# The first round of a top-32 search, over 144 columns instead of 168

## The chip, the cores and the metric

The kernel runs on one core of one Trainium2 chip, in float32. Its metric is the device time of one execution in microseconds (us). The engines are called PE (TensorE), DVE (VectorE), ACT (ScalarE), POOL (GpSimd) and SP (SyncE); PEld is the weight loading of PE.

## The reference

Attention that keeps, for each query, only the scores that reach its 32nd largest one, and then a layer of experts in which each token goes to one expert.

```python
scores = scale * np.matmul(q, k.transpose(0, 1, 3, 2))      # B, H, S, D = 8, 8, 576, 64
kth = np.partition(scores, -32, axis=-1)[..., -32:-31]
scores = np.where(scores >= kth, scores, -1e9)
attn = softmax(scores)
x = np.matmul(attn, v)                                      # to 4608 rows of 512
expert = np.argmax(x @ w_gate, axis=1)                      # 8 experts
y = np.maximum(x @ w1[expert], 0) @ w2[expert]              # 512 -> 1024 -> 512
out = gate_weight[:, None] * y
```

## The kernel before

**The steps.** A tile is 128 queries of one head against its 576 keys. The attention is a list of 144 steps (`work`); a step handles two tiles (index `m`), 18 steps make a batch, and 8 batches follow each other. The main loop (from L916) goes over the steps under an order of PE, ACT and DVE that is written out by hand; SP and POOL follow the order of the program. Work is staggered: PE multiplies queries and keys (L276) and ACT copies the scores to `s` (L283) three steps ahead, so four buffers of `s` are in turn; DVE folds the scores of step i + 1 while it searches step i; PE transposes the weights of step i - 1 (`transposed`, L398 to L419).

**The search.** What DVE must find is the 32nd largest of 576 scores per query. First the scores are folded. `fold` (L290, L292) takes the larger and the smaller of each two scores, into `h` and `l` (288 columns each). `fold_on` (L298, L300) does the same once more with `h`: the larger ones go to the first 144 columns of `few` (QF = 144), the smaller ones to `hl`. `few` has 168 columns (LW): behind the 144 lie three lists of eight, the eight largest of `l` and of each half of `hl` (MAX8, L329). Whatever is among the 32 largest of the tile is then among the 168, unless a list was too short; `doubts` (L360, on POOL) compares the last entry of each list with the threshold, and in the rare case an exact path at the end of the program does all again.

`search` then takes four rounds of eight. In each, MAX8 (L338) writes the eight largest values of its source to `tops`; after each but the last, MATCH_REPLACE8 (L345, with a MATCH_VALUE_LOAD of the eight values in front of it) puts a very low number in their places. Before the change round 0 reads all 168 columns of `few` and the replacement writes to `scr`; rounds 1 to 3 read `scr`. Both tiles of a step go through each round one after the other. Before the last scan the loop calls `fold_on` for the next step (`then`). The threshold is the last of the 32 values.

**What follows a search.** ACT turns the thresholds into `low` (L354), then makes from `s` a huge number where a score lies under the threshold (`depths`, L370); POOL subtracts that from the scores (`less`, L379); ACT takes the exponential with its sum (`weights`, L387), with a bias that POOL made from the first maximum (`nbias`, L342). PE transposes the weights in the next step and ACT copies them out (L402 to L419). Every few steps PE multiplies them with the values (L432), ACT copies the result (L434), PE turns it to rows (L443), ACT copies it (L450), ACT and DVE make the divisors (`rz`, L454 to L457), and POOL multiplies rows by divisors (L478). At the end of a batch small DVE operations choose experts and places (L488 to L534) and a table of blocks (L587 to L626); they are put between the scans one at a time (`tick`).

**The experts.** From the second batch on, pieces of expert blocks (L687, L702) are put into PE's order between the attention's steps, as many at each step as a credit allows; it counts steps and blocks, not time. The blocks that are left over run after the attention, on PE almost alone.

**Buffers.** `few` has three, `scr` one, `s` four. DVE's instructions run in their order; semaphores of DVE's own guard a value that its next instruction reads.

Of the kernel before, what the change touches and what calls it, by code (L numbers as in the profile page):

```python
# [30 lines left out]
def _inner(ap: bass.AP, n: int) -> bass.AP:  # L31
    return _ins(ap, len(ap.ap), n)
# [3 lines left out]
def kernel(  # L36
# [6 lines left out]
    moe_w2: bass.AP,  # L43
    out: bass.AP,
):

# [46 lines left out]
    QF = S // 4  # L95
# [23 lines left out]
    k = SimpleNamespace()  # L119
# [48 lines left out]
    for odd in range(2):  # L168
        for h in range(2):
            r = slice(h * D, (h + 1) * D)  # L170
# [63 lines left out]
    def in_turn(put):  # L234

        if not k.exact:
            tc.keep_in_program_order(put)
        return put
# [11 lines left out]
    def tails(tiles):  # L250
        return tiles[0][1] == 2 * NC
# [52 lines left out]
    def tick():  # L304

        while aside:
            if next(aside[0], "end") != "end":
                return
            aside.pop(0)
# [7 lines left out]
    def search(tiles, s, f, then=lambda: None):  # L317

        m_all = range(2)
        tops = k.small.tile([P, 2, TOP_K], F32, name="tops", bufs=4)  # L320
        if k.exact:
            src = [s[:, m, :, :].rearrange("p j k -> p (j k)") for m in m_all]
            width = S
        else:
            src = [f.few[:, m, :] for m in m_all]
            width = LW
            for m in m_all:
                for j, away in enumerate((f.l[:, m, :], f.hl[:, m, 0:QF // 2], f.hl[:, m, QF // 2:QF])):
                    nc.vector.max(out=f.few[:, m, QF + 8 * j:QF + 8 * j + 8], in_=away)  # L329
        scr = k.att.tile([P, 2, width], F32, name="scr", bufs=1)  # L330
        nbias = k.small.tile([P, 2], F32, name="nbias", bufs=3)
        R = TOP_K // 8

        for r in range(R):
            if r == R - 1:
                then()
            for m in m_all:
                nc.vector.max(out=tops[:, m, r * 8:(r + 1) * 8], in_=src[m])  # L338
                if r:
                    tick()  # L340
            if r == 0:
                in_turn(nc.gpsimd.tensor_scalar_mul(nbias, tops[:, :, 0], -scale))  # L342
            if r < R - 1:
                for m in m_all:
                    nc.vector.match_replace(  # L345
                        out=scr[:, m, :], in_to_replace=tops[:, m, r * 8:(r + 1) * 8],
                        in_values=src[m], imm_value=NEG,
                    )
                    if r:
                        tick()  # L350
                    src[m] = scr[:, m, :]
        thr = tops[:, :, TOP_K - 1]
        low = k.small.tile([P, 2], F32, name="low", bufs=3)
        nc.scalar.activation(low, thr, AF.Copy, scale=STEEP)  # L354

        def doubts():
            n, i = tiles[0]
            at = n.b * U + n.u
            over = doubt[:, at:at + 2, 2 * NC, :] if tails(tiles) else doubt[:, at, 2 * i:2 * i + 2, :]
            k.last_pool = in_turn(nc.gpsimd.tensor_tensor(  # L360
                over, f.few[:, :, QF + 7:LW:8], _inner(thr, NL), op=ALU.subtract
            )).ins

        return low, nbias, doubts
# [115 lines left out]
    def choice(lg):  # L480

        r = SimpleNamespace(lg=lg)
        mx = k.small.tile([P, KC], F32, name="mx")
        r.oh = oh = k.small.tile([P, KC, E], F32, name="oh")
        idx = k.small.tile([P, KC], F32, name="idx")

        def steps():
            nc.vector.tensor_reduce(mx, lg, axis=AX.X, op=ALU.max)  # L488
            yield
            nc.vector.tensor_tensor(oh, lg, _inner(mx[:, :], E), op=ALU.is_ge)  # L490
            yield
            nc.vector.tensor_tensor(oh, oh, _ins(e_less[:, :], 1, KC), op=ALU.mult)
            yield
            nc.vector.tensor_tensor(lg, lg, _inner(mx[:, :], E), op=ALU.subtract)
            yield
            nc.vector.tensor_reduce(idx, oh, axis=AX.X, op=ALU.min)
            yield
            nc.vector.tensor_tensor(oh, e_same, _inner(idx[:, :], E), op=ALU.is_equal)
            yield

        r.steps = steps()
        return r
# [231 lines left out]
    with fast:  # L734
# [171 lines left out]
        def loop():  # L906
# [9 lines left out]
            for i, (b, g) in enumerate(work):  # L916
# [8 lines left out]
                if i + 1 < len(work):  # L925
                    f_of[i + 1] = fold(s_of[i + 1])
                    then = lambda: fold_on(f_of[i + 1])
                low, nbias, doubts = search(tiles, s_of[i], f_of.pop(i), then)
                at_place("small")
                w_of[i] = depths(s_of[i], low)  # L930
# [73 lines left out]
    with ExitStack() as outer:  # L1004
# [10 lines left out]
        with ExitStack() as st:  # L1015
# [7 lines left out]
            with tc.For_i(0, B, 1) as b:  # L1023
# [3 lines left out]
                for u in range(0, U, 2):  # L1027
                    two = [load_unit(b, u), load_unit(b, u + 1)]
                    for n in two:
                        load_values(n)  # L1030
                        open_unit(n)
                    for g in groups(u):
                        tiles = [(two[a - u], tile) for a, tile in g]
                        s, steps = scores(products(tiles))
                        for step in steps:
                            step()
                        low, nbias, _ = search(tiles, s, None)
                        w = depths(s, low)
                        less(s, w)
                        weights(tiles, w, nbias)  # L1040
                        for _ in transposed(tiles, w):
                            pass
                        n, tile = tiles[0]
                        if tile == (NC - 1 if n.u % 2 else 2 * NC):
                            for _ in outputs(n, x):
                                pass
                            for _ in divisors(n):
                                pass
                            logits(n, lg)
                            rows(n, x)  # L1050
                r = choice(lg)
# [68 lines left out]
```

## Time and profile before

| what | us |
|---|---|
| median of 6 runs | 1373.19 (1371.40 to 1375.38) |
| the profiled execution | 1374.58 |
| its span, first to last instruction | 1373.0 |
| PE busy | 1234.4 (90%) |
| PE weight loads | 837.8 (61%) |
| DVE busy | 1085.7 (79%) |
| ACT busy | 931.2 (68%) |
| POOL busy | 661.1 (48%) |

Busy times are shares of the whole span. The attention fills roughly the first four fifths of it and the experts that are left the last fifth, in which DVE has next to nothing to do, so 79% of the span is nearly all of the attention. A group of instructions is told as its line, engine, operation, output and input with their shapes, and count, then the busy time in us and the mean length of one in ns, then the idle time of the engine ahead of it. Instructions of DVE overlap a little: the next one starts before the one ahead of it is shown as ended.

### The profile page before, as it was taken

Reading aid. Unit: us, or ns where it says so; the run is one execution under the profiler, and the core shown is the slowest. Engines: PE = TensorE matmul, PEld = TensorE weight load, DVE = VectorE, ACT = ScalarE, POOL = GpSimd, SP = SyncE. Lnnn points to the kernel's source line nnn. Section 1 sums busy time; section 2 is a strip of 40 time slices with the busy share of each in tenths; the row PEclk is TensorE's granted clock in tenths of the full one; section 3 lists DMA queues with packets and bytes.
Section 4 is the critical chain, followed back from the end, with each engine's and each line's share of the span. In section 5 each row is a group of like instructions: output and inputs, shape, how many; then the busy total and the mean of one; then the engine's idle time right before and its main releaser. Section 6 shows DMA issues by size and latency. Waiting matters only on the chain. (4 is left out here: it accounts for less than half of the span.)

```text
span 1373.0 us, 24487 instructions
## 1 busy us (share of the span) xinstructions
PE 1234.4 (90%) x7666; PEld 837.8 (61%) x7666; DVE 1085.7 (79%) x4591; ACT 931.2 (68%) x2113; POOL 661.1 (48%) x805
## 2 busy tenths in 40 slices
PE   5777677677799999999999999999999999999995
PEld 3444444344466666766666666767676676776773
DVE  8999999999999999999999999999999820000000
ACT  4788877877888888888877788887777821111110
POOL 3454557555654666566556656565557621000000
PEclk9788887887899999999999999999999999999998
DMA  2000011001583267427654474357542759999890
GB/s 82 29 29 29 28 36 55 29 29 44 179 290 122 94 231 266 140 73 255 232 176 166 168 274 145 113 190 296 178 167 88 294 182 361 385 322 331 302 320 18
DMA packets 102220, 231.68 MB, mean 169 GB/s; under 512 B 5182, under 2 KB 25918, under 8 KB 102080
## 3 DMA queue, kind: packets, MB, share of 16 engines
q1 hardware_dynamic: 95328, 209.76, 43.5%
q0 software_dynamic: 6464, 19.97, 4.0%
q8 instruction: 62, 1.02, 0.3%
q14 instruction: 78, 0.64, 0.1%
q10 hardware_dynamic: 288, 0.30, 0.1%
HBM read 208.72 MB, written 22.33 MB: 168 GB/s over the span
## 5 line engine op out<-in xcount | busy, mean ns | idle before, releaser
L379 POOL TENSOR_TENSOR w<-s,w 128x576 f32<-128x576 f32 x288 | 409.1, 1440 | 433.7 <-ACT w L370 433.7
L687 PE MATMUL ph<-xTs,w 128*128 128x128 f32 x2560 | 308.6, 276 | 6.7 <-ACT xTs L664 6.0
L687 PEld LDWEIGHTS ph<-xTs,w 128*128 128x128 f32 x2560 | 297.4, 192 | 27.3 <-issue 19.9
L702 PE MATMUL py<-w,hT 128*128 128x512 f32 x640 | 292.2, 596 | 0.0
L338 DVE MAX8 tops<-scr 128x8 f32<-128x168 f32 x864 | 247.8, 320 | 0.0
L276 PE MATMUL sc<-qkb 64*128 64x288 f32 (+1 forms) x1280 | 223.0, 474 | 9.6 <-ACT s L283 5.2
L387 ACT ACTIVATE w<-w,nbias 128x576 f32<-128x576 f32 x288 | 224.1, 792 | 3.5 <-POOL w L379 2.5
L370 ACT ACTIVATE w<-s,low 128x576 f32<-128x576 f32 x288 | 207.6, 768 | 4.7
L398 PE MATMUL wTm<-turn,w 128*128 128x128 f32 x1152 | 170.9, 288 | 28.9 <-ACT xl L450 17.1
L999 DVE CAST any_i<-pd 1x1 int32<-1x1 f32 x1 | 0.1, 146 | 237.2 <-PE pd L997 237.2
L398 PEld LDWEIGHTS wTm<-turn,w 128*128 128x128 f32 x1152 | 132.7, 146 | 89.7 <-issue 36.2
L702 PEld LDWEIGHTS py<-w,hT 128*128 128x128 f32 x640 | 114.4, 190 | 117.6 <-issue 116.5
L345 DVE MATCH_REPLACE8 scr<-tops,scr 128x168 f32<-128x168 f32 x576 | 178.4, 316 | 0.0
L283 ACT COPY s<-sc 128x576 f32<-128x576 f32 x288 | 169.0, 641 | 11.2 <-PE sc L276 11.2
L404 ACT COPY wT<-wTm 128x512 f32<-128x512 f32 x256 | 139.1, 604 | 38.9 <-PE wTm L398 38.7
L276 PEld LDWEIGHTS sc<-qkb 64*128 64x128 f32 (+1 forms) x1280 | 119.0, 197 | 73.7 <-issue 27.0
L432 PE MATMUL po<-wT,vb 128*64 128x288 f32 x1024 | 156.9, 455 | 0.4 <-ACT wTt L419 0.4
L708 POOL DMA_INDIRECT out_dram<-y,xg x40 | 43.1, 1077 | 212.7 <-ACT y L716 199.7
L329 DVE MAX8 few<-l 128x8 f32<-128x288 f32 x288 | 128.8, 447 | 0.0
L432 PEld LDWEIGHTS po<-wT,vb 128*64 128x64 f32 x1024 | 75.2, 152 | 78.5 <-issue 29.0
L290 DVE TENSOR_TENSOR h<-s 128x576 f32<-128x576 f32 x144 | 118.4, 822 | 5.9 <-ACT s L283 5.9
L692 ACT ACTIVATE hT<-ph 128x512 f32<-128x512 f32 x80 | 48.6, 608 | 108.3 <-PE ph L687 108.2
(116 smaller groups left out, 1441.0 us busy)
## 6 DMA issues: line engine op xcount, KB each, us to landing
w<-in_moe_w_dram SPq DMA_DIRECT2D x80, 2048.0 KB, 9.5
qkb<-in_qk_dram SPq DMA_DIRECT2D x31, 608.0 KB, 4.1
xg<-x_rows SPq DMA_DIRECT2D x40, 257.0 KB, 9.7
vb<-in_v_dram SPq DMA_DIRECT2D x32, 320.0 KB, 3.3
x_rows<-blank SPq DMA_DIRECT2D x5, 257.0 KB, 15.5
x_rows<-blank POOLq DMA_DIRECT2D x4, 257.0 KB, 9.2
x_rows<-x,posi POOLq DMA_INDIRECT x40, 3.3
out_dram<-y,xg POOLq DMA_INDIRECT x40, 6.1
```

The lines of the kernel that those rows point to most:

```text
L276: nc.tensor.matmul(ps[rows, j, 0:HF], n.q[d, cols], n.k[d, keys], start=True, stop=True)
L283: lambda m=m, ps=ps: nc.scalar.copy(s[:, m, :, :], ps[:, :, 0:HF]) for m, ps in enumerate(got)
L338: nc.vector.max(out=tops[:, m, r * 8:(r + 1) * 8], in_=src[m])
L345: nc.vector.match_replace(out=scr[:, m, :], in_to_replace=tops[:, m, r * 8:(r + 1) * 8], in_values=src[m], imm_value=NEG,)
L370: nc.scalar.activation(w[:, m, :], s[:, m, :, :].rearrange("p j k -> p (j k)"), AF.Relu, scale=-STEEP, bias=low[:, m:m + 1],)
L379: k.last_pool = in_turn(nc.gpsimd.tensor_tensor(w[:, m, :], s[:, m, :, :].rearrange("p j k -> p (j k)"), w[:, m, :], op=ALU.subtract)).ins
L387: nc.scalar.activation(w[:, m, :], w[:, m, :], AF.Exp, scale=scale, bias=nbias[:, m:m + 1], accum_out=n.z[:, c:c + 1])
L398: nc.tensor.transpose(pm[:, c * P:(c + 1) * P], w[:, m, first:first + P], ident)
L404: nc.scalar.copy(wT[:, :, m, q], pm4)
L432: nc.tensor.matmul(po[r, 0:HF], n.v[:, c, r], rhs, start=(c == 0), stop=(c == KC - 1))
L687: nc.tensor.matmul(ph[:, f, :], n.w1[:, 0, dt, fc * P:(fc + 1) * P], n.xT[:, dt, :], start=(dt == 0), stop=(dt == DT - 1),)
L702: nc.tensor.matmul(py, hT[:, f, :], n.w2[:, 0, f, :], start=(f == 0), stop=(f == FT - 1))
```

## The change

In round 0 the scan reads only the 144 folded columns of `few`, without the three lists, and the replacement, over the same 144 columns, writes into `few` in place. Round 1 then reads all 168 columns of `few`, where the lists now come in, and replaces from `few` to `scr`; rounds 2 and 3 go on in `scr` as before. The exact path is as it was. At least eight of the folded columns hold one of the tile's 32 largest scores, since a column stands for four scores, so the first eight values taken are among the 32 in either order and the threshold is the same.

```diff
-            src = [f.few[:, m, :] for m in m_all]
+            src = [f.few[:, m, 0:QF] for m in m_all]
             width = LW
 ...
             if r < R - 1:
                 for m in m_all:
+                    first = r == 0 and not k.exact
                     nc.vector.match_replace(
-                        out=scr[:, m, :], in_to_replace=tops[:, m, r * 8:(r + 1) * 8],
+                        out=src[m] if first else scr[:, m, :], in_to_replace=tops[:, m, r * 8:(r + 1) * 8],
                         in_values=src[m], imm_value=NEG,
                     )
                     if r:
                         tick()
-                    src[m] = scr[:, m, :]
+                    src[m] = f.few[:, m, :] if first else scr[:, m, :]
```

## The prediction

> **What bounds the kernel now.** I read the page's slices first: which engine is full, and when.
>
> ```profile
> PE   5777677677799999999999999999999999999995
> ...
> DVE  8999999999999999999999999999999820000000
> ...
> PEclk9788887887899999999999999999999999999998
> ```
>
> VectorE (DVE) is full until the attention ends near 1094 us. TensorE (PE) has room at first; from about 385 us, when expert blocks are mixed into the attention, both are full. So second, the groups of instructions, for what DVE is full of:
>
> ```profile
> L338 DVE MAX8 tops<-scr 128x8 f32<-128x168 f32 x864 | 247.8, 320 | 0.0
> ...
> L329 DVE MAX8 few<-l 128x8 f32<-128x288 f32 x288 | 128.8, 447 | 0.0
> ...
> L329 DVE MAX8 few<-hl 128x8 f32<-128x72 f32 x576 | 101.1, 217 | 0.0
> L345 DVE MATCH_REPLACE8 scr<-tops,few 128x168 f32<-128x168 f32 x288 | 89.1, 316 | 0.0
> L338 DVE MAX8 tops<-few 128x8 f32<-128x168 f32 x288 | 79.4, 317 | 0.0
> ```
>
> Scans and replacements, with no idle time before them. The last two rows are what the change shortens: 288 of each, two per search, 144 searches. Third, the waits, for who follows whom. ScalarE (ACT) makes `low` (L354) as soon as a search has its threshold, and the rest of a step follows from `low`: depths, subtraction, weights, transposes, outputs. So I asked where ACT stood idle before `low`:
>
> ```profile
> ACT low L354 <- DVE tops L338: 60.9, 55, 4.2
> ...
> DVE rz L457 <- ACT rz L455: 10.9, 7, 6.0
> ...
> DVE h L290 <- ACT s L283: 5.9, 6, 1.5
> ```
>
> By window the first row splits into 54.0 us in 45 waits before 491 us, 3.5 in 5 in 491 to 625, none in 625 to 876, 3.5 in 5 in 876 to 906, none after. Where ACT waits, DVE sets the pace; where it does not, ACT and PE lag behind and DVE runs ahead, until it must itself wait for ACT. In the order of time around the second group (start, length, wait in brackets):
>
> ```profile
> 868.95 0.20 ACT L354 ACTIVATE low<-tops 128x2 f32<-128x2 f32 x1
> ...
> 876.40 0.20 ACT L354 ACTIVATE low<-tops 128x2 f32<-128x2 f32 x1 [0.21 <-DVE tops L338]
> ...
> 883.96 0.21 ACT L354 ACTIVATE low<-tops 128x2 f32<-128x2 f32 x1 [0.18 <-DVE tops L338]
> ...
> 891.58 0.20 ACT L354 ACTIVATE low<-tops 128x2 f32<-128x2 f32 x1 [1.66 <-DVE tops L338]
> ```
>
> Last, the stretches that these waits mark (length, then busy us of PE, weight loads, DVE, ACT, POOL; clock):
>
> ```profile
> 0.00:491.00 491.00, 382.79 (x2237) 239.72 (x2239) 484.21 (x2083) 388.79 (x895) 264.21 (x347) 0.86 0.23 79
> 491.00:625.00 134.00, 130.81 (x874) 90.20 (x872) 133.87 (x572) 113.33 (x261) 81.95 (x97) 1.00 0.51 179
> 625.00:876.00 251.00, 247.44 (x1647) 171.83 (x1646) 246.39 (x1014) 204.28 (x467) 148.25 (x171) 1.00 0.56 201
> ...
> 1094.00:1345.00 251.00, 248.38 (x1452) 180.81 (x1451) 9.02 (x46) 46.02 (x85) 28.53 (x35) 1.00 0.85 302
> ```
>
> **What one search saves.** In round 0 the scan and the replacement read 144 columns instead of 168. MAX8 has three widths: (320 - 217) / 96 = 1.07 ns and (447 - 320) / 120 = 1.06 ns a column, so 24 columns are 25.5 ns. In the timeline two scans of 72 columns start 0.13 us apart and two of 168 columns 0.23, also 1.0 ns a column, so the saving is in the pace and not only in the length. The replacement has no row at another width. Bounds: nothing, and its full share, 316 x 24 / 168 = 45 ns; nearest is MAX8, 320 ns beside 316 at the same width, so 25.5. One search saves 4 x 25.5 = 102 ns; all 144, 14.7 us of DVE time.
>
> **What comes with it, at nothing.** The replacement now writes into `few` itself. In place costs no more: `scr` from `scr` (rounds 1 and 2) has the same 316 ns as `scr` from `few`. `MATCH_VALUE_LOAD` (76 ns) keeps its eight values. The second round reads `few` where it read `scr`: 168 columns either way. POOL's `doubt` (L360) reads the lists in `few`, which the new write leaves alone, and it waits for the threshold, which is later. `few` has three buffers, and its last reader stays `doubt`. The value load of round 0 waits for its scan: the second scan will start 0.21 us after the first and the load 0.21 after that, when the first scan (0.29) is 0.13 over; dependent small operations at the start of the trace follow each other in 0.03, so no wait opens. The first scan needs the lists no more, but they stay ahead of it in DVE's order: no gain, no loss.
>
> **How much of it reaches the end.** A search counts where ACT waits for it, or where its lead is handed over at a later wait.
> - Up to the wait at 490 us: 66 searches, 6.7 us. Off goes 0.1 for each of the 11 searches in which a fold is held by POOL's row product (L478; `few` at L298 then lasts up to 1.40 us for 0.45): it ends when POOL lets go, however early it came. 5.6 left.
> - 491 to 625: 18 searches. ACT lags by up to 2.7 us, but DVE never stops, and its lead comes through at the five waits of 595 to 625 (0.21, 0.18, 1.66, 0.99, 0.44): 1.8, less two held folds, 1.6.
> - 625 to 906: 36 searches, but DVE stops five times for ACT, last at 796 us (`rz`, 0.68). What it had gained by then is given up there. The 14 searches from there to 906 make 1.4, which fits under the 1.66.
> - 906 to 1094: no wait of ACT for `tops`, three of DVE's for `rz` and two for `h`. ACT and PE set the pace; 24 searches bring nothing.
>
> After 1094 us PE alone is left (248.38 of 251 us busy), unchanged and earlier. Sum: 5.6 + 1.6 + 1.4 = 8.6 us. The profiled execution took 1374.58 us (span 1373.0), 1.4 above the median of 1373.19; 8.6 off gives 1366.0 for it and **1364.6 us** on the median's footing.
>
> **Two rules against rows.** Is PE full from 491 us on? Its matmul row says 247.44 of 251. Its weight loads say 171.83 of 251, 68%, where the tail, with nothing to wait for, has 72%: about 5% of room, and by the waits it lies around 600 and 890. The Trainium skill (Perfetto Trace Analysis, Identifying the Most-Contended Engine) calls matmul busy time no good measure and the weight-load share a good one; taken by itself it would let PE follow everywhere, 14.7 us, and the matmul row would stop the gain at about 385 us.
>
> Against the change stands this row: `h` of 0.73 us took 1.69 beside a subtraction of POOL's, and ended 0.62 after that one.
>
> ```profile
> 735.28 1.41 POOL L379 TENSOR_TENSOR w<-s,w 128x576 f32<-128x576 f32 x1
> 735.62 1.69 DVE L290 TENSOR_TENSOR h<-s 128x576 f32<-128x576 f32 x1
> ```
>
> The Trainium skill (SBUF — State Buffer, Who interferes with whom) states that a VectorE instruction with two SBUF inputs and a GpSimd one that reads SBUF shut each other out, while one-input instructions are free. By it the shortened scans are safe, but the folds behind them come earlier and may meet POOL more often; if every search met it, the gain would be gone, 1373.2.
>
> **Rivals.**
> - All of it reaches the end (PE has the room and DVE's stops shrink): 14.7 us, 1358.5. For it, the weight loads; against it, DVE's own stops after 660 us. 0.14.
> - PE is full from 385 us on, and only the 53 searches before it count: 5.4 less 0.9 for held folds, 1368.7. For it, the matmul row; against it, ACT's waits at 595 to 625, when PE stands still too. 0.19.
> - Slower, by POOL's lock. Up to 491 us `low` follows `tops` at once and the subtraction (L379) falls on the one-input scans; if the shorter search shifts it or the row product onto a fold, that costs up to 0.95 us each time (1.69 - 0.74; 1.40 - 0.45). From 9 new full hits the gain is gone; at 15 the time is 1364.6 + 14.2 = 1379. Against it: both move with the search they follow, and 0.1 us is little beside scans of several us. 0.09.
> - It does not do what it says: instructions no shorter by 24 columns, or a new wait in front of the second round that eats them; 1373. The three widths speak against it. With a few new hits that just cancel the gain, 0.08.
>
> **Numbers.** Forecast 0.50. A difference under about 0.2% (2.7 us) can't be told from none here. Faster: 0.50 + 0.14 + 0.19 = 0.83; same 0.08; slower 0.09. The range takes in the first two rivals, the replacement's bounds (0 to 45 ns: 8.6 becomes about 4.3 to 12) and one or two hits each way: 1357.5 to 1371.
>
> **What would show it.** Scans of 128x144 at 291 to 295 ns and replacements of 128x144 near 290, 288 each, with the remaining rows at 320 and 316; DVE busy 1071 instead of 1085.7; attention ending near 1085 us instead of 1094, with a tail of the same 251 us; ACT's waits for `low` shorter in the groups at 595 and 876, DVE's waits for `h` and `rz` longer. Wrong would be: replacements still at 316 (4.3 us of gain), folds (L290, L298, L300) longer on the mean than 822, 535 and 484 ns, or the groups of ACT waits gone altogether, which would mean that ACT and PE set the pace from there on.

## The result, and the profile after

The changed kernel takes 1369.88 us (median of 17 runs, 1366.60 to 1372.71) beside 1373.35 us of the kernel before (39 runs): ratio 0.9975, 95% interval 0.9969 to 0.9982, or 2.5 to 4.3 us less. A second comparison gave 0.9962 (0.9949 to 0.9976). So it is faster by a little, 3.5 to 5.3 us by the two comparisons, where 8.6 had been forecast. The profiled execution took 1368.68 us (span 1367.1).

The shortened instructions came out as costed. Groups of the changed kernel, shapes apart:

```profile
L347 DVE MATCH_REPLACE8 scr<-tops,few 128x168 f32<-128x168 f32 x288 | 89.2, 316 | 0.0
...
L339 DVE MAX8 tops<-few 128x8 f32<-128x168 f32 x288 | 83.7, 318 | 0.0
L347 DVE MATCH_REPLACE8 few<-tops,few 128x144 f32<-128x144 f32 x288 | 81.9, 291 | 0.0
L339 DVE MAX8 tops<-few 128x8 f32<-128x144 f32 x288 | 72.2, 292 | 0.0
```

Each lost 25 ns, the replacement too, in place and all. The waits of the changed kernel (us in total, times, longest) show DVE stopping more often for ACT:

```profile
ACT low L356 <- DVE tops L339: 56.2, 51, 4.1
...
DVE rz L459 <- ACT rz L457: 13.7, 14, 6.0
...
DVE h L291 <- ACT s L284: 7.0, 6, 1.6
```

`rz` had 7 such waits and has 14. DVE's busy time fell from 1085.7 to 1076.8 us, not to the 1071 that the scans and replacements alone would give. Other instructions became longer, most of all the fold into `few` (552 ns on the mean for 535, 2.4 us in all), and the waits for `rz` and `h` grew by 3.9 us (13.7 for 10.9, 7.0 for 5.9).

Where the time went is read from `low` (ACT, L354 before, L356 after), the first thing that follows a search. For searches 66 and 144 the timelines of ACT have, before and after:

```profile
490.44 0.20 ACT L354 ACTIVATE low<-tops 128x2 f32<-128x2 f32 x1 [0.45 <-DVE tops L338]
...
1093.32 0.22 ACT L354 ACTIVATE low<-tops 128x2 f32<-128x2 f32 x1
```

```profile
485.32 0.20 ACT L356 ACTIVATE low<-tops 128x2 f32<-128x2 f32 x1 [0.24 <-DVE tops L339]
...
1088.16 0.22 ACT L356 ACTIVATE low<-tops 128x2 f32<-128x2 f32 x1
```

Up to search 66 the changed kernel gains 5.12 us. From there to search 144 it takes 602.84 us, where the kernel before takes 602.89: 78 searches, by the lengths above 8.0 us less of DVE's scans and replacements, and 0.05 us less of time. The same two distances for all the kernels (us; "rest" runs from search 144 to the end of the span):

| kernel | to search 66 | 66 to 144 | rest |
|---|---|---|---|
| before | 490.44 | 602.89 | 279.66 |
| after | 485.32 | 602.84 | 278.92 |
| after, once more | 485.12 | 602.89 | 279.69 |
| short round early | 485.39 | 603.18 | 279.81 |
| short round late | 492.00 | 602.65 | 279.02 |
| two rounds | 480.95 | 602.62 | 278.92 |
| no subtraction, before / after | 483.80 / 479.19 | 600.87 / 601.21 | 278.72 / 277.93 |
| half products, before / after | 488.64 / 484.60 | 571.43 / 568.22 | 279.93 / 280.31 |
| half products, short round late | 487.91 | 568.30 | 278.40 |
| no sums, before / after | 489.28 / 485.23 | 603.31 / 602.67 | 278.59 / 278.23 |
| two rounds, guarded | 482.91 | 602.93 | 279.70 |

Two kernels with the same instructions up to search 66 differ there by 1.6 us (before, and short round late), and the rest lies anywhere from 277.9 to 280.3 us, for reasons that no run here settles. The middle repeats best.

### The profile page after: what moved, and what is told of

The parts are those of the page before. It is cut to its first block, busy times and chain, and to the rows that moved or that the text cites. A ratio compares the mean times of both kernels' runs of the same rounds, so it can differ in the third digit from the quotient of the medians.

```text
span 1367.1 us, 24487 instructions
## 1 busy us (share of the span) xinstructions
PE 1227.7 (90%) x7666; PEld 835.1 (61%) x7666; DVE 1076.8 (79%) x4591; ACT 931.4 (68%) x2113; POOL 668.4 (49%) x805
## 5 line engine op out<-in xcount | busy, mean ns | idle before, releaser
L284 ACT COPY s<-sc 128x576 f32<-128x576 f32 x288 | 169.1, 641 | 10.9 <-PE sc L277 10.9
L339 DVE MAX8 tops<-scr 128x8 f32<-128x168 f32 x576 | 164.0, 321 | 0.0
L339 DVE MAX8 tops<-few 128x8 f32<-128x144 f32 (+1 forms) x576 | 155.9, 305 | 0.0
L434 PE MATMUL po<-wT,vb 128*64 128x288 f32 x1024 | 151.5, 442 | 0.4 <-ACT wTt L421 0.4
```

What stands on the lines that cost most here:

```text
L284: lambda m=m, ps=ps: nc.scalar.copy(s[:, m, :, :], ps[:, :, 0:HF]) for m, ps in enumerate(got)
L434: nc.tensor.matmul(po[r, 0:HF], n.v[:, c, r], rhs, start=(c == 0), stop=(c == KC - 1))
```

## The experiments

The theory I began with was that DVE's lead after 491 us is given up where POOL's reading holds a fold (called held folds). The rivals were that ACT and PE set the pace there whatever DVE does (pace), and that every search is simply worth less (even).

**Where the searches count.** Two kernels use the short round in one part of the attention each:

```diff
+        searched.append(1)
+        short = not k.exact and len(searched) <= 66      # the other kernel: > 66
...
-            src = [f.few[:, m, 0:QF] for m in m_all]
+            src = [f.few[:, m, 0:QF if short else LW] for m in m_all]
...
-                    first = r == 0 and not k.exact
+                    first = r == 0 and short
```

> The short first round in searches 1 to 66 only (up to about 491 us), the old one from 67 on. Theory (held folds): after 491 us DVE's lead is given up at the next fold that POOL's reading holds, because POOL's place is set by ACT; so all of the change's gain is made here: the time equals that of the whole change, 3 to 4 us under the kernel before (ratio 0.9975), and the last threshold comes about 5 us earlier in the trace. Rival (even): each search brings the same, about 0.024 us of the 3.5: 1.6 us under, last threshold under 2.5 us earlier. The forecast on record would have 5.6 us here.

Measured: 1368.88 us against 1374.48 of the kernel before on the same chip, ratio 0.996 (0.9947 to 0.9973), and search 144 is 4.75 us earlier in the trace.

> The old first round in searches 1 to 66, the short one from 67 on. Theory (held folds): no more than 0.3 us under the kernel before, with DVE ahead by 0.1 us a search in the trace until a held fold, then level again. Rival (even): 1.9 us under. The forecast on record: 3.0 us under (1.6 and 1.4).

Measured: 1373.24 against 1374.48, ratio 0.9995 (0.9986 to 1.0003); from search 66 to 144, 602.65 us for 602.89. The early part has the whole gain, which puts "even" aside; the forecast's 3.0 us of the late part are not there. In the trace DVE does get ahead: beside `low`, its fold into `l` (L292 of the kernel before) starts 0.24 us earlier in search 70 than it did. In search 72 the two are level again.

**A second dose.** Round 1 also reads 144 columns in place:

```diff
-                    first = r == 0 and not k.exact
+                    first = r < 2 and not k.exact
...
-                    src[m] = f.few[:, m, :] if first else scr[:, m, :]
+                    src[m] = (f.few[:, m, :] if r else f.few[:, m, 0:QF]) if first else scr[:, m, :]
```

> Rounds 0 and 1 both over 144 columns in place, the lists come in at round 2: 0.2 us of DVE per search instead of 0.1. Theory (held folds, and ACT's own pace after 491 us): the second 0.1 us counts again only up to 491 us and less there, as ACT's waits of 0.1 to 1 us for the threshold are used up: 2.5 to 5 us under the whole change (6 to 8.5 under the kernel before), and between 491 us and the end of the attention nothing more than before. Rival (even): 3.5 us more, spread evenly, half of it after 491 us.

Measured: 1364.79 us, ratio 0.9935 (0.9922 to 0.9948), 4.1 us under the early kernel on the same chip. All of it is made before search 66 (480.95); from there on 0.2 us of DVE time per search, 15.6 in all, change 602.89 to 602.62.

**Held folds, or the pace of PE and ACT.** The subtraction is POOL's longest work. Two kernels leave it out, one from each side of the change:

```diff
-            k.last_pool = in_turn(nc.gpsimd.tensor_tensor(
-                w[:, m, :], s[:, m, :, :].rearrange("p j k -> p (j k)"), w[:, m, :], op=ALU.subtract
-            )).ins
+            pass
...
-                w[:, m, :], w[:, m, :], AF.Exp, scale=scale, ...
+                w[:, m, :], w[:, m, :], AF.Exp, scale=-scale, ...
```

> The kernel before without POOL's subtraction (L379): the exponential is taken of ACT's depths with the sign turned, so weights are wrong. It takes away 409 us of POOL work and with it the reading that holds DVE's folds; POOL's row products (L478) stay. ACT waited only 2.5 us for the subtraction, so it gains little by that. Theory (held folds): the folds L290, L298, L300 fall from 822, 535, 484 ns to near 760, 480, 455; the time falls by 3 to 8 us, since after 491 us ACT and PE set the pace in any case. Rival (ACT and PE have no room at all): under 2 us.

> The changed kernel without the subtraction, to be read against the one before it. Theory (held folds): with the holds gone DVE keeps its lead from one group of ACT's waits to the next, and the change is worth what the forecast gave it, 8 to 10 us between the two. Rival (pace): ACT and PE set the pace from 491 us on whether folds are held or not; the change is worth 3.5 to 6 us as with the subtraction, and DVE's waits for h and rz grow in place of the holds.

Measured: 1364.66 and 1360.06 us (ratios to the kernel before 0.9937, 0.9923 to 0.9950, and 0.9904, 0.9889 to 0.9919). The change is worth 4.6 us between them, all of it by search 66; the middle, from search 66 to 144, is 600.87 and 601.21 us. My theory expected 8 to 10, the rival 3.5 to 6: my theory falls. The holds did go. Groups of the kernel before without the subtraction:

```profile
L290 DVE TENSOR_TENSOR h<-s 128x576 f32<-128x576 f32 x144 | 113.4, 788 | 10.4 <-ACT s L283 10.4
...
L298 DVE TENSOR_TENSOR few<-h 128x288 f32<-128x288 f32 x144 | 65.8, 457 | 0.0
L300 DVE TENSOR_TENSOR hl<-h 128x288 f32<-128x288 f32 x144 | 64.3, 447 | 0.0
```

They were 822, 535 and 484 ns, and in place of the holds DVE stops more for ACT: 10.4 us for `h` where it had been 5.9. More telling is what became of ACT's waits for a threshold from 491 to 1094 us, before and then without the subtraction:

```profile
ACT low L354 <- DVE tops L338: 7.0, 10, 1.7
```

```profile
ACT low L354 <- DVE tops L338: 1.2, 4, 0.4
```

These ten waits were the forecast's evidence that DVE sets the pace there. Without POOL's subtraction six of the ten are gone. The timeline of the kernel before shows how the first group starts:

```profile
589.09 2.79 POOL L379 TENSOR_TENSOR w<-s,w 128x576 f32<-128x576 f32 x2 [3.97 <-ACT w L370]
...
590.70 1.20 DVE L591 TENSOR_SCALAR ci<-ci 1x8 int32<-1x8 int32 x1
...
595.44 0.20 ACT L354 ACTIVATE low<-tops 128x2 f32<-128x2 f32 x1 [0.21 <-DVE tops L338]
```

POOL's subtraction waits for ACT (in brackets), DVE's small operation of eight numbers is held until POOL is done at 591.88, and the threshold then comes 0.21 us late for ACT. A faster scan ahead of the hold moves nothing: its end is set by ACT. In the changed kernel that wait is still 0.20 us:

```profile
590.54 0.20 ACT L356 ACTIVATE low<-tops 128x2 f32<-128x2 f32 x1 [0.20 <-DVE tops L339]
```

Behind the hold the shorter scans do count, but not for long. At search 80, the one above, the changed kernel is 4.90 us earlier; at searches 82, 83 and 84 it is 5.04, 5.14 and 5.25 us earlier, 0.1 us more each time, as the forecast has it. Then comes ACT's next wait, for PE. Search 84 and this wait, before and after:

```profile
624.74 0.21 ACT L354 ACTIVATE low<-tops 128x2 f32<-128x2 f32 x1 [0.44 <-DVE tops L338]
...
627.27 0.89 ACT L450 COPY xl<-px 128x432 f32<-128x432 f32 x2 [0.86 <-PE px L443]
```

```profile
619.49 0.20 ACT L356 ACTIVATE low<-tops 128x2 f32<-128x2 f32 x1 [0.24 <-DVE tops L339]
...
622.23 0.89 ACT L452 COPY xl<-px 128x432 f32<-128x432 f32 x2 [1.06 <-PE px L445]
```

ACT waits 0.20 us less for DVE and then 0.20 us longer for PE; `xl` and the next threshold come 5.04 and 5.03 us earlier. The group at 876 us repeats this (5.03, 5.37, then 5.15).

So the rival holds: ACT and PE set the pace. Which of the two?

**PE.** Half of the first expert products are left out while they are mixed into the attention; the tail keeps them:

```diff
-                for dt in range(DT):
+                some = DT if k.exact or k.apart else DT // 2
+                for dt in range(some):
```

> The kernel before with half of the first expert products (two of four slices of the contraction) left out wherever expert work is mixed into the attention; the tail is whole. PE has some 80 us less to do before 1094 us. Both theories: ACT no longer lags, DVE sets the pace nearly to the end, the time falls by 20 to 50 us.

> The changed kernel with the same part left out, read against the one before it. Theory (ACT and PE's lag behind is what lets the folds be held): with the lag gone 0.1 us a search counts to the end: 10 to 14 us between the two. Rival (even, the saving is worth 0.024 us a search wherever it is): 3 to 4 us between the two.

Measured: 1341.47 and 1331.68 us (ratios to the kernel before 0.9763, 0.9750 to 0.9777, and 0.9693, 0.9677 to 0.9710): with room on PE the change is worth 9.8 us, more than twice as much. That is just short of the 10 to 14 expected, and the runs of the changed kernel lie from 1328.5 to 1334.8 us, so its size is rough; the two traces have 6.9 us between their spans, with 3.2 us from search 66 to 144. ACT's waits for the threshold from 491 to 1094 us say why, before and after:

```profile
ACT low L354 <- DVE tops L338: 31.3, 42, 1.7
```

```profile
ACT low L356 <- DVE tops L339: 23.0, 32, 1.6
```

Now ACT waits in more than half of the steps, and the shorter search takes 8.3 us of these waits away.

> Half of the first expert products left out inside the attention, as in the runs on PE's room, with the old first round up to search 66 and the short one from 67 on. Theory (late searches count as soon as PE has room): 3 to 7 us under the kernel before with the same part left out (1341.47). Rival (late searches never count, as DVE is held by POOL or stopped by rz all the same): under 1 us.

Measured: 1336.21 us, 5.3 under the same kernel with the old round, which ran on another chip (the kernel before took 1373.84 us on this one and 1373.37 on that). In the traces 3.1 us of it lie between search 66 and 144, 568.30 us for 571.43. The late searches, worth nothing in the full kernel, count as soon as PE has room.

**ACT.** The sum behind each exponential is left out:

```diff
-                w[:, m, :], w[:, m, :], AF.Exp, scale=scale, bias=nbias[:, m:m + 1], accum_out=n.z[:, c:c + 1]
+                w[:, m, :], w[:, m, :], AF.Exp, scale=scale, bias=nbias[:, m:m + 1]
...
         n.z = k.small.tile([P, NT], F32, name="z")
+        nc.gpsimd.memset(n.z, 1.0)
```

> The kernel before without the sum that ACT reads out after each exponential (288 readings of 211 ns, 60.7 us of ACT); the sums are set to one, so rows are scaled wrongly. Theory (PE sets the pace from 491 us on, ACT only follows PE): under 8 us faster, since ACT's freed 0.4 us a step becomes waiting for PE. Rival (ACT sets it): 78 steps of 0.42 us, 25 to 33 us faster.

> The changed kernel without that reading, against the one before it. Theory (PE sets the pace): the change is worth 3.5 to 6 us, as with the reading. Rival (ACT sets it): with ACT out of the way DVE sets the pace to the end and the change is worth 9 us or more.

Measured: 1372.88 us, ratio 0.9997 (0.9988 to 1.0006), and 1368.04 us with the change, 4.8 less. The relief is smaller than the 60.7 us of the expectation: the readings overlap the exponentials, and ACT's busy time fell by 23 us, from 931.2 to 908.1. So the 25 to 33 us that the rival was to bring were too many; by the windows below, ACT has 13 us less to do in the middle, and the middle is no shorter (603.31 us for 602.89). From 491 to 1094 us, the windows of the kernel before and of the one without the sums (length, busy PE, weight loads, DVE, ACT, POOL):

```profile
491.00:1094.00 603.00, 590.61 (x3914) 408.93 (x3913) 592.10 (x2461) 494.48 (x1132) 366.94 (x423) 1.00 0.54 193
```

```profile
491.00:1094.00 603.00, 590.04 (x3908) 408.62 (x3908) 592.14 (x2458) 481.35 (x975) 361.44 (x441) 1.00 0.54 194
```

ACT's column falls, PE's stays at 98% of the time. What ACT saves it spends waiting, mostly for PE: its waits for PE's product `po` (L432), for example, grow from 20.9 to 25.8 us. Work taken off PE, 73 us of its busy time (1234.4 to 1161.1), had made the program 32 us shorter. So PE sets the pace of the middle.

**A version for use.** Two short rounds are right only if the first 16 values taken are among the 32 largest of the tile, that is, if 16 columns hold one. This kernel checks it and falls back on the exact path; its later rounds use `l` in place of `scr`:

```diff
-        scr = k.att.tile([P, 2, width], F32, name="scr", bufs=1)
+        scr = k.att.tile([P, 2, width], F32, name="scr", bufs=1) if k.exact else f.l[:, :, 0:width]
...
+            in_turn(nc.gpsimd.tensor_tensor(
+                over[:, :, 0:NL], f.few[:, :, QF + 7:LW:8], _inner(thr, NL), op=ALU.subtract
+            ))
             k.last_pool = in_turn(nc.gpsimd.tensor_tensor(
-                over, f.few[:, :, QF + 7:LW:8], _inner(thr, NL), op=ALU.subtract
+                over[:, :, NL], thr, tops[:, :, 15], op=ALU.subtract
             )).ins
```

> A version for use: rounds 0 and 1 over 144 columns in place; POOL also compares the 16th value taken with the threshold and sends the program to its exact path when it is smaller, one operation of 128x2 more per search (about 0.2 us of POOL, off the path); rounds 2 and 3 replace into the folded low halves, which are read out by then. Theory: as two rounds without the guard, 1363.5 to 1367, 7 to 10 us under the kernel before. Rival (the added operation meets DVE's folds): 1367 or more.

Measured: 1366.98 us, ratio 0.9952 (0.9938 to 0.9965): faster than the kernel before, and a little faster than the changed one, though its interval overlaps the second one of that (0.9949 to 0.9976). It is about 2.2 us behind the one without the check. Search 66 ends 2.0 us later than there (482.91 for 480.95), and `h` means 850 ns for 808. That is not the rival as it was put: up to 490 us eight `h` take 1.33 us or more, where the kernel without the check has four, and all of them lie beside POOL's row product (L478 of the kernel before), none beside the added operation. Whether that operation moved the row product there or the use of `l` did, no run tells.

**The size of the gain.**

> The changed kernel once more, unaltered, for how far the gain itself scatters. If the trace's 5.2 us at the end of the attention is what the change is worth: 4.5 to 6 us under the kernel before on the same chip. If the 3.5 us of the first comparison is: 2.5 to 4.3. In its trace, search 66 may end 1 to 2 us away from 485.3 us, since the same instructions differed by 1.6 us there between two runs (490.4 and 492.0), and the distance from there to the last threshold should be 601.8 us as before within 0.2.

Measured: 1369.46 us against 1374.76, ratio 0.9962 (0.9949 to 0.9976), 5.3 us; search 66 at 485.12 and 602.89 us from there to search 144. The trace repeats to 0.2 us (the 601.8 us of the expectation is not the distance of the first trace, which is 602.84). The two comparisons agree only between 0.9969 and 0.9976, 3.3 to 4.3 us; why the first lies at the low end stays open.

## Why the prediction was right and wrong

**Right.** The cost of one search: 25 ns for each of the four instructions, for scan and replacement alike, no dearer in place, and no new wait in round 0. The early part: 5.6 us forecast, 5.12 in the trace, 4.0 to 5.3 over the pairs of kernels that differ by the change; as the same instructions differed there by 1.6 us, this is agreement only within that. The last part: nothing from 906 us on.

**Wrong.** The terms of 1.6 us (491 to 625) and 1.4 us (625 to 906) are nothing: together 3.0 us forecast, 0.05 in the trace. The step that failed is "its lead comes through at the five waits", and with it the 1.4 us that were to fit under the second group of waits. The lead from before each group was gone by its first wait, and of the 0.35 us made inside it 0.22 went to ACT's next wait for PE. I took a wait of ACT for `tops` as proof that DVE sets the pace at that place. But at the first wait DVE was late because POOL had held it, and POOL had been waiting for ACT. A chain that goes back to ACT by way of POOL looks, in the list of waits, like a wait for DVE. And ACT, in its turn, follows PE there, as the runs with less work on PE show. I counted as DVE's stops only its waits for semaphores (`h`, `rz`); a hold is shown as a longer instruction, not as idle time, so it escaped that count, although I had used holds elsewhere at 0.1 us each. Held folds are not the whole of it, though: without POOL's subtraction the change is worth no more after 491 us (600.87 and 601.21 us).

The sign that the prediction named for this case, the groups of ACT's waits gone altogether, did not come: eight of the ten waits are still there in the changed kernel, and yet PE sets the pace.

The rival "PE is full from 385 us on" named 1368.7 us and the matmul row as its evidence. The median came to 1369.88. Its sum, 4.5 us by search 53, fits the trace as well: search 53 comes at 389.23 us for 393.70, 4.47 earlier, and 0.65 us more is gained from there to search 66. I had argued against it with the same waits.

**The two rules.** The Trainium skill (Perfetto Trace Analysis, Identifying the Most-Contended Engine) prefers the weight-load share (and the rate of useful arithmetic) to the matmul share, as a measure of how much room TensorE has. Here the weight loads stood at 408.93 of 603 us, 68%, while PE set the pace; the room that this share suggests was of no use to the shorter search, and what takes it up no run here shows. The matmul row, 590.61 of 603, told in this case which engine was full. The Trainium skill (SBUF — State Buffer, Who interferes with whom) says that a VectorE instruction with two SBUF inputs contends with a GpSimd one that reads SBUF. The runs agree: the folds `few` and `hl` fall to 457 and 447 ns when POOL's subtraction is gone. With one input it calls an instruction free only outside the modes that use both ports, a condition that the prediction left out; the shortened scans and replacements did stay free. But taking the holds away wins the change nothing after 491 us.

## What to carry to other kernels

Before a saving on one engine is carried through a wait of another, follow that wait back past the engine it names: if the named engine had itself been held or slowed by something that depends on the waiter, the wait is an echo and not a price. Follow the saving forward too: what is gained at one wait can be lost at the next, as 0.20 us were here. Count instructions that last longer than their kind as stops too, beside the idle times. And where two engines are both full, take work off each in turn, as these runs did with ACT and PE: the one whose relief moves the time sets the pace. Compare how much busy time each relief really took away.

## What the runs showed of the hardware

A small DVE operation with a single input is held by POOL as well: the shift of eight integers (L591) means 419 ns, up to 1.20 us beside POOL's subtraction, and 145 ns in the kernel without it. `MAX8` and `MATCH_REPLACE8` keep their 316 to 321 ns on the mean at 168 columns in the changed kernel and in the kernel before, 312 to 317 ns in the latter without POOL's subtraction, and 314 to 319 ns in the changed kernel run once more. So no hold of theirs shows.
